# First image of an attention and feed-forward kernel: chunk-wise pipeline of four tiles, values turned from keys, staged weights, lag of three

## The chip, the cores and the metric

One core of one Trainium2 chip. The metric is the device time of one execution in microseconds; lower is better. "Span" is the time from the first to the last instruction in a profiled execution, about 2 us less than the device time. TensorE is called PE, VectorE DVE, ScalarE ACT, GpSimd POOL; SP is the engine that issues most DMAs. "Clock" is the share of TensorE's full speed that was granted, as a mean over the run or over a stretch; "half rate" is a time in which it was half. To "turn" is to transpose.

## The reference, cut to what matters

```python
# q (4, 12288, 128), kv (4, 384, 32, 128), w_sr (128, 128); all fp32
kv_pool = kv.reshape(B, H // 4, 4, W // 4, 4, C).mean(axis=(2, 4))   # 768 keys per image
k = v = kv_pool.reshape(B, -1, C) @ w_sr                             # keys and values are the same
a = softmax(q @ k.T / sqrt(128))                                     # per image
x = (a @ v).reshape(49152, 128)
out = (maximum(x @ w_gate, 0) * (x @ w_val)) @ w_out                 # hidden width 1536
```

The kernel works on 96 tiles of 512 tokens, 24 per image. The 768 keys of an image come in six chunks of 128, each pooled from 1.05 MB of kv. A tile needs 6 score matmuls, 24 value matmuls, 12 + 12 feed-forward projections and 48 output matmuls.

## The kernel before

First the start, for image 0. Each chunk is pooled (DVE), turned (PE), projected twice (once for keys, once for values, both in fp32) and scored against four tiles; values of two tiles follow one chunk later.

```python
def project(b, jc, kvT, copy):
    pr = bank([128, 2, 128])
    nc.tensor.matmul(pr[:, 0, :], w_sr_f32, kvT, start=True, stop=True)   # keys, channels by keys
    nc.tensor.matmul(pr[:, 1, :], kvT, w_sr_f32, start=True, stop=True)   # values, keys by channels
    copy(kv16[:, b, jc, 0 : 2 * C], pr.rearrange("p i c -> p (i c)"))

# start
for jc in range(NJC):                                    # NJC = 6
    s1 = pool_lines(nc.vector, 0, jc, nc.gpsimd if jc in (3, 4) else None)
    if jc == 3:
        q_load(1)                                        # second query group: casting DMA from GpSimd
    if jc == 4:
        # ... casting DMAs of w_val, w_gate, w_out, all from GpSimd ...
    if jc == 0:
        q_turn_pe(0)                                     # fp32 turns on PE
    kvT = turn_pooled(s1, nc.scalar.copy)
    if jc > 0:
        # ... values of tiles 0 and 1 for chunk jc - 1 ...
    project(0, jc, kvT, act_scaled)
    for k in range(GRP):                                 # GRP = 4
        if jc == 0 and k > 0:
            q_turn_pe(k)
        scores(k, jc)
q_turn(1)                                                # DMA transpose of the second query group
q_load(2)
# ... last values of tiles 0, 1; all values of tile 2; x_turn_pe(0), x_turn_pe(1) ...
for jc in range(NJC):
    scores(GRP, jc)                                      # needs the second query group
    values(3, jc, 0)
# ... rest of values of tile 3 ...
```

The main loop then works on tile k's scores, tile k - 1's values, the projections of tile k - LAG and the output of tile k - LAG - 1 at once, in 12 steps:

```python
for k in range(LEAD, last + 1):                          # LEAD = LAG = 5
    for step in range(NFB):                              # NFB = 12
        kO, kF = k - LAG - 1, k - LAG
        if 0 <= kO: out_proj(kO, step)
        if 0 <= kF < NT: value_proj(kF, step)
        # ... scores(k, ..) on even steps, values(k - 1, ..) on odd ones ...
        if 0 <= kF < NT: gate_proj(kF, step)
        # ... in the last tiles of an image: load, pool, turn and project the next image's chunks ...
```

The softmax here doesn't subtract the row's maximum and nothing guards it: scores larger than these inputs give would overflow.

Of the kernel before, what the change touches and what calls it, by code (L numbers as in the profile page):

```python
# [16 lines left out]
def kernel(  # L17
# [38 lines left out]
    LEAD = GRP + 1  # L56
    LAG = LEAD
# [39 lines left out]

    def q_turn_pe(i):
        q32 = q32s.pop(i)
        qt_ps = bank([128, NS, 128])  # L100
        for s in range(NS):
            nc.tensor.matmul(
                qt_ps[:, s, :], q32[:, s, :], ident, is_transpose=True, start=True, stop=True
            )
        if i == 0:
            qTs[0] = work.tile([128, GRP * NS, 128], FP16, tag="qT", bufs=3, name="qT")
        nc.vector.tensor_copy(qTs[0][:, i * NS : (i + 1) * NS, :], qt_ps)
# [21 lines left out]
    def pool_lines(eng, b, jc, other=None):  # L129
        parts = kv_in.pop((b, jc))  # L130
        s2 = work.tile([128, 2, r, C], FP32, tag="kv_s2")
        for i in range(2):
            (other if i and other else eng).tensor_tensor(  # L133
                s2[:, i], parts[:, 2 * i], parts[:, 2 * i + 1], op=ALU.add
            )
        s1 = work.tile([128, r, C], FP32, tag="kv_s1")
        eng.tensor_tensor(s1, s2[:, 0], s2[:, 1], op=ALU.add)  # L137
        return s1
# [8 lines left out]
    def turn_pooled(pooled, copy):  # L147
        tp = bank([128, 128])
        n = pooled.shape[1]
        for i in range(n):  # L150
            nc.tensor.matmul(  # L151
                tp, pooled[:, i, :], ident, is_transpose=True,
                start=(i == 0), stop=(i == n - 1),
            )
        kvT = work.tile([128, 128], FP32, tag="kvT")
        copy(kvT, tp)
        return kvT

    def project(b, jc, kvT, copy):
        pr = bank([128, 2, 128])  # L160
        nc.tensor.matmul(pr[:, 0, :], w_sr_f32, kvT, start=True, stop=True)  # L161
        nc.tensor.matmul(pr[:, 1, :], kvT, w_sr_f32, start=True, stop=True)  # L162
        copy(kv16[:, b, jc, 0 : 2 * C], pr.rearrange("p i c -> p (i c)"))

    def act_scaled(dst, src):
        nc.scalar.mul(dst, src, 1.0 / (r * r))

    def dve_scaled(dst, src):
        nc.vector.tensor_scalar(dst, src, 1.0 / (r * r), None, op0=ALU.mult)
# [5 lines left out]
    def scores(k, jc):  # L175
        if jc == 0:
            aTs[k] = work.tile([128, NJC, T], FP16, tag="aT", bufs=5, name="aT")
# [4 lines left out]
    def values(k, jc, half, turn=True):  # L182
# [13 lines left out]
        if jc == NJC - 1:  # L196
# [7 lines left out]
            if half == 1 and turn:  # L204
                x16 = x16s.pop(k)
                xT = work.tile([128, NS, 128], FP16, tag="xT", bufs=8, name="xT")
                nc.sync.dma_start_transpose(xT, x16.rearrange("p s c -> p (s c)"))
                xTs[k] = xT.rearrange("c s p -> c (s p)")

    def x_turn_pe(k):  # L210
# [4 lines left out]
        xT = work.tile([128, NS, 128], FP16, tag="xT", bufs=8, name="xT")  # L215
# [74 lines left out]
    wo16 = const.tile([128, NFB, 128], FP16)  # L290

    for jc in range(NJC):
        s1 = pool_lines(nc.vector, 0, jc, nc.gpsimd if jc in (3, 4) else None)
        if jc == 3:
            q_load(1)
        if jc == 4:
            for own in (slice(0, D_FF // 2), slice(D_FF // 2, D_FF)):
                nc.gpsimd.dma_start(wv16[:, own], moe_w_val[:, own])
                nc.gpsimd.dma_start(wg16[:, own], moe_w_gate[:, own])
            nc.gpsimd.dma_start(wo16, moe_w_out.rearrange("(fb f) c -> f fb c", f=128))  # L300
        if jc == 0:
            q_turn_pe(0)
        kvT = turn_pooled(s1, nc.scalar.copy)
        if jc > 0:
            for k in range(2):
                for half in range(2):
                    values(k, jc - 1, half, turn=False)
        project(0, jc, kvT, act_scaled)
        for k in range(GRP):
            if jc == 0 and k > 0:  # L310
                q_turn_pe(k)
            scores(k, jc)
    q_turn(1)
    q_load(2)
# [3 lines left out]
    for jc in range(NJC):  # L318
        values(2, jc, 0)
    for k in range(2):  # L320
        x_turn_pe(k)
    for jc in range(NJC):
        values(2, jc, 1)
    for jc in range(NJC):
        scores(GRP, jc)
        values(3, jc, 0)
    for jc in range(NJC):
        values(3, jc, 1)
# [4 lines left out]
    for k in range(LEAD, last + 1):  # L333
# [6 lines left out]
        for step in range(NFB):  # L340
            kO, kF = k - LAG - 1, k - LAG
            if 0 <= kO:
                out_proj(kO, step)
            if 0 <= kF < NT:
                value_proj(kF, step)
            if step % 2 == 0:
                if k < NT:
                    scores(k, step // 2)
            elif k - 1 < NT:
                half, i = divmod(step // 2, NJC // 2)  # L350
                values(k - 1, 2 * i, half)
                values(k - 1, 2 * i + 1, half)
            if 0 <= kF < NT:
                gate_proj(kF, step)
            if b < B:
# [4 lines left out]
                if step == 7 and 0 <= at - 4 < NJC:  # L360
                    kv_Ts[b, at - 4] = turn_pooled(kv_s3.pop((b, at - 4)), nc.vector.tensor_copy)
                if step == 9 and 0 <= at - 4 < NJC:
                    project(b, at - 4, kv_Ts.pop((b, at - 4)), dve_scaled)
# [34 lines left out]
```

## Time and profile before

| | before |
|---|---|
| device time, median of 4 runs | 1077.57 us (1073.12 to 1079.37) |
| span of the profiled run | 1071.8 us |
| first feed-forward matmul | 55.47 us |
| PE's wait for the turned second query group | 5.1 us, until 51.51 |
| one steady tile | 10.47 us, PE busy 10.47 |

The span consists of a start, in which PE has gaps, and a long rest, in which it has none. So the table is read as a sum: first feed-forward matmul at 55.47, and 1016.3 us from there. The lines for it stand in the prediction below; its 55.63 is where the chain of waits takes that matmul up, while PE's timeline has it start at 55.47. Two lines of the timeline of the kernel before (start, duration, engine, source line, operation, count, and in brackets the idle time before and what ended it) show how a chunk is paced there: the exponentials of four tiles come every 3.89 us.

```profile
30.94 2.06 ACT L180 ACTIVATE aT<-bank_ps 128x512 f16<-128x512 f32 x4 [0.48 <-PE bank_ps L179]
...
34.83 2.06 ACT L180 ACTIVATE aT<-bank_ps 128x512 f16<-128x512 f32 x4 [0.48 <-PE bank_ps L179]
```

2.06 us for four is the rate when PE delivers at full clock.

### The profile page before, as it was taken

The page shows a single profiled execution, that of the slowest core. Times are in us where ns is not written, and L with a number is a line of the kernel's source. Part 1 is how long each engine was busy: PE and PEld are TensorE (multiplying, and loading weights), DVE is VectorE, ACT ScalarE, POOL GpSimd, SP SyncE. Part 2 cuts the span into 40 slices and gives each one's busy share as a digit, 9 for nine tenths or more (in the row PEclk, how much of TensorE's full clock was granted, in tenths as well). Part 3 has the DMA queues.
Part 4 walks back from the last instruction along what each step waited for, and adds up shares of the span by engine and source line. Part 5 has one row for each costly group of instructions (what it writes and reads, how often), then busy time and mean ns, then how long its engine had stood idle before and what let it go on. Part 6 is the DMA issues. An engine that isn't in the chain of part 4 may idle for free.

```text
span 1071.8 us, 26152 instructions
## 1 busy us (share of the span) xinstructions
PE 1040.3 (97%) x9954; PEld 692.8 (65%) x9954; DVE 925.5 (86%) x1782; ACT 913.3 (85%) x1762; POOL 109.7 (10%) x128
## 2 busy tenths in 40 slices
PE   4699999999999999999999999999999999999997
PEld 2466666666666666666666666666666666666664
DVE  3388989898989889989888898988888889898896
ACT  1598888888888888888888888888888888888887
POOL 1200054200000015400000004420000000000000
PEclk9999999999999999999999999999999999999999
DMA  9953356341431447524313237643132232121111
GB/s 257 130 84 60 84 147 164 81 85 31 85 68 47 80 108 169 129 51 84 71 45 82 54 65 168 143 110 79 37 84 51 65 71 59 37 65 32 44 41 41
DMA packets 132911, 90.76 MB, mean 85 GB/s; under 512 B 104113, under 2 KB 104753, under 8 KB 132785
## 3 DMA queue, kind: packets, MB, share of 16 engines
q1 hardware_dynamic: 127344, 75.85, 31.3%
q0 software_dynamic: 5440, 13.24, 7.8%
q8 instruction: 78, 1.28, 0.5%
q14 instruction: 49, 0.39, 0.1%
HBM read 52.76 MB, written 25.17 MB: 73 GB/s over the span
## 4 chain that ended last, share of the span: by engine, by line
PE 94%; DMA 4%; ACT 0%; SPq 0%; DVE 0%; POOL 0%; issue 0%; ACTq 0%; POOLq 0%; DVEq 0%
PE bank_ps L246 24%; PE bank_ps L232 23%; PE bank_ps L221 23%; PE bank_ps L191 12%; PE bank_ps L179 11%; DMA parts<-in_kv_dram 2%; DMA qT<-q 2%; DMA q<-in_q_dram 1%; PE bank_ps L162 0%; PE bank_ps L161 0%; DVE hT L235 0%; PE bank_ps L151 0%; ACT o_sb L256 0%; POOL s L133 0%; SPq L124 0%
## 5 line engine op out<-in xcount | busy, mean ns | idle before, releaser
L235 DVE SCALAR_TENSOR_TENSOR hT<-bank_ps,val 128x512 f16<-128x512 f32 x1152 | 763.1, 686 | 102.0 <-ACT val L225 68.0
L225 ACT CAST val<-bank_ps 128x512 f16<-128x512 f32 x1152 | 677.4, 591 | 119.3 <-PE bank_ps L221 116.2
L246 PEld LDWEIGHTS <-hT 128*128 128x128 f16 x4608 | 351.8, 98 | 206.5 <-DVE hT L235 2.9
L246 PE MATMUL bank_ps<-wo,hT 128*128 128x128 f16 x4608 | 443.4, 219 | 2.1 <-DVE hT L235 2.0
L221 PE MATMUL bank_ps<-xT,wv 128*128 128x512 f16 x1152 | 436.6, 379 | 0.0
L232 PE MATMUL bank_ps<-xT,wg 128*128 128x512 f16 x1152 | 435.7, 378 | 0.3 <-DVE hT L235 0.3
L180 ACT ACTIVATE aT<-bank_ps 128x512 f16<-128x512 f32 x576 | 345.7, 604 | 15.8 <-PE bank_ps L179 15.7
L179 PE MATMUL bank_ps<-qT,kv 128*128 128x512 f16 x576 | 218.0, 383 | 10.3 <-DMA qT<-q 5.1
L191 PE MATMUL bank_ps<-kv,aT 128*128 128x129 f16 x2304 | 224.2, 220 | 0.1
L191 PEld LDWEIGHTS <-aT 128*128 128x128 f16 x2304 | 177.8, 98 | 68.1 <-issue 1.3
L232 PEld LDWEIGHTS <-wg 128*128 128x128 f16 x1152 | 111.5, 97 | 64.4
L221 PEld LDWEIGHTS <-wv 128*128 128x128 f16 x1152 | 112.7, 98 | 0.9 <-issue 0.5
L198 DVE CAST x<-bank_ps 128x256 f16<-128x256 f32 x192 | 79.4, 414 | 18.4 <-PE bank_ps L191 18.4
L78 POOL DMA_DIRECT2D q<-in_q_dram x23 | 12.7, 550 | 543.4 <-DMA qT<-q 543.2
L133 POOL TENSOR_TENSOR s<-parts 128x512 f32<-128x512 f32 x38 | 49.0, 1291 | 180.9 <-DMA parts<-in_kv_dram 119.0
L179 PEld LDWEIGHTS <-kv 128*128 128x128 f16 x576 | 56.4, 99 | 11.6 <-DMA qT<-q 5.2
L258 DVE TENSOR_TENSOR o_sb<-bank_ps,inv 128x512 f32<-128x512 f32 x91 | 61.9, 680 | 0.0
L199 DVE RECIPROCAL rinv<-bank_ps 128x2 f32<-128x2 f32 x192 | 30.5, 159 | 0.0
L137 POOL TENSOR_TENSOR s<-s 128x512 f32<-128x512 f32 x18 | 22.9, 1270 | 1.4
L203 DVE TENSOR_TENSOR inv<-rinv 128x4 f32<-128x4 f32 x96 | 19.0, 198 | 3.3
L133 DVE TENSOR_TENSOR s<-parts 128x512 f32<-128x512 f32 x10 | 8.8, 901 | 8.3 <-DMA parts<-in_kv_dram 8.3
L151 PE MATMUL bank_ps<-ident,s 128*128 128x128 f32 x42 | 9.7, 308 | 5.9 <-DVE s L137 5.7
(33 smaller groups left out, 108.9 us busy)
## 6 DMA issues: line engine op xcount, KB each, us to landing
parts<-in_kv_dram SPq DMA_DIRECT2D x96, 256.0 KB, 5.0
out_dram<-o_sb SPq DMA_DIRECT2D x96, 256.0 KB, 2.2
q<-in_q_dram POOLq DMA_DIRECT2D x23, 512.0 KB, 5.2
xT<-x SPq DMA_TRANSPOSE x94, 2.5
q<-in_q_dram SPq DMA_DIRECT2D x4, 256.0 KB, 5.9
wv<-in_moe_w_val_dram POOLq DMA_DIRECT2D x2, 192.0 KB, 5.4
wg<-in_moe_w_gate_dram POOLq DMA_DIRECT2D x2, 192.0 KB, 5.8
wo<-in_moe_w_out_dram POOLq DMA_DIRECT2D x1, 384.0 KB, 17.5
```

What stands on the lines that cost most here:

```text
L133: (other if i and other else eng).tensor_tensor(s2[:, i], parts[:, 2 * i], parts[:, 2 * i + 1], op=ALU.add)
L179: nc.tensor.matmul(s_ps, kv16[:, k // NST, jc, 0:C], qT_of(k), start=True, stop=True)
L180: nc.scalar.activation(aTs[k][:, jc, :], s_ps, AF.Exp, scale=qk_scale)
L191: nc.tensor.matmul(x_ps[:, i, :], aTs[k][:, jc, s * 128 : (s + 1) * 128], kv16[:, k // NST, jc, C : 2 * C + 1], start=(jc == 0 and i == 0) ...
L198: nc.vector.tensor_copy(x16s[k][:, own, :], x_ps[:, :, 0:C])
L199: nc.vector.reciprocal(rinvs[k][:, own], x_ps[:, :, C])
L221: nc.tensor.matmul(va_ps, wv16[:, fb * 128 : (fb + 1) * 128], xTs[k], start=True, stop=True)
L225: nc.scalar.copy(val, va_ps)
L232: nc.tensor.matmul(g_ps, wg16[:, fb * 128 : (fb + 1) * 128], xTs[k], start=True, stop=True)
L235: nc.vector.scalar_tensor_tensor(hTs[k][:, fb, :], g_ps, 0.0, vals.pop((k, fb)), op0=ALU.max, op1=ALU.mult)
L246: nc.tensor.matmul(o_ps[:, s, :], hTs[k][:, fb, s * 128 : (s + 1) * 128], wo16[:, fb, :], start=(fb == 0 and s == 0), stop=(fb == NFB - 1) ...
L258: nc.vector.tensor_tensor(o_sb, o_ps, inv2.to_broadcast([128, NS, 128]), op=ALU.mult)
```

## The change

Its intent is to let the feed-forward begin sooner. Image 0 runs chunk by chunk with the queries cast to fp16 on ACT before they are turned; one of the three additions that pool a chunk's lines goes to GpSimd (before, only for two chunks); keys alone are projected and the values are the same numbers turned by a cheap fp16 transpose; the weights come as plain fp32 DMAs from SP right behind kv and are cast by GpSimd; and the feed-forward starts when only four tiles are scored, with a lag of three instead of five. The core of the diff:

```diff
-    LEAD = GRP + 1
-    LAG = LEAD
+    LAG = GRP - 1
...
-    def project(b, jc, kvT, copy):
-        pr = bank([128, 2, 128])
-        nc.tensor.matmul(pr[:, 0, :], w_sr_f32, kvT, start=True, stop=True)
-        nc.tensor.matmul(pr[:, 1, :], kvT, w_sr_f32, start=True, stop=True)
-        copy(kv16[:, b, jc, 0 : 2 * C], pr.rearrange("p i c -> p (i c)"))
+    def project(b, jc, kvT):
+        pr = bank([128, 128])
+        nc.tensor.matmul(pr, w_sr_f32, kvT, start=True, stop=True)
+        nc.vector.tensor_scalar(
+            kv16[:, b, jc, 0:C], pr, 1.0 / (r * r), None, op0=ALU.mult
+        )
+    def turn_values(b, jc):
+        vt = bank([128, 128], FP16)
+        nc.tensor.transpose(vt, kv16[:, b, jc, 0:C], ident16)
+        nc.vector.tensor_copy(kv16[:, b, jc, C : 2 * C], vt)
...
+        w32 = work.tile([128, 2, HF], FP32, tag="kv_in", bufs=6, name="w32")
+        for n, (w16, w) in enumerate(((wv16, moe_w_val), (wg16, moe_w_gate))):
+            nc.sync.dma_start(w32[:, n], w[:, own])
...
     for jc in range(NJC):
-        s1 = pool_lines(nc.vector, 0, jc, nc.gpsimd if jc in (3, 4) else None)
+        s1 = pool_lines(nc.vector, 0, jc, nc.gpsimd)
+        kvT = turn_pooled(s1)
...     (values of tile 0 for chunk jc - 1)
+        project(0, jc, kvT)
...     (values of tile 1 for chunk jc - 1)
         for k in range(GRP):
             scores(k, jc)
+            if k == 0:
+                turn_values(0, jc)
+    q_load(1)
     q_turn(1)
+    for w16, w32 in staged:
+        nc.gpsimd.tensor_copy(w16, w32)
     q_load(2)
...
+            if k == LAG:                    # first feed-forward tile: values of tiles 2 and 3
+                for jc in (2 * i, 2 * i + 1):
+                    values(k - 1 + step % 2, jc, half)
```

More of the change, by code (lines that the diff above doesn't have):

```diff
@@ L96, in q_load_plain, with q_cast @@
         q32s[i] = q32
+    def q_cast(i):
+        q16 = work.tile([128, NS, C], FP16, tag="q16s", bufs=2, name="q16s")
+        nc.scalar.copy(q16, q32s[i])
+        q16s[0, i] = q16
     def q_turn_pe(i):
-        q32 = q32s.pop(i)
-        qt_ps = bank([128, NS, 128])
+        q16 = q16s.pop((0, i))
+        qt_ps = bank([128, NS, 128], FP16)
         for s in range(NS):
-            nc.tensor.matmul(
-                qt_ps[:, s, :], q32[:, s, :], ident, is_transpose=True, start=True, stop=True
-            )
+            nc.tensor.transpose(qt_ps[:, s, :], q16[:, s, :], ident16)
         if i == 0:
@@ L132, in pool_lines @@
         for i in range(2):
-            (other if i and other else eng).tensor_tensor(
+            (other if i == 0 and other else eng).tensor_tensor(
                 s2[:, i], parts[:, 2 * i], parts[:, 2 * i + 1], op=ALU.add
@@ L145, in pool_columns, with turn_pooled @@
         return s3
-    def turn_pooled(pooled, copy):
+    def turn_pooled(pooled):
         tp = bank([128, 128])
@@ L155, in turn_pooled @@
         kvT = work.tile([128, 128], FP32, tag="kvT")
-        copy(kvT, tp)
+        nc.vector.tensor_copy(kvT, tp)
         return kvT
-    def project(b, jc, kvT, copy):
-        pr = bank([128, 2, 128])
-        nc.tensor.matmul(pr[:, 0, :], w_sr_f32, kvT, start=True, stop=True)
-        nc.tensor.matmul(pr[:, 1, :], kvT, w_sr_f32, start=True, stop=True)
-        copy(kv16[:, b, jc, 0 : 2 * C], pr.rearrange("p i c -> p (i c)"))
-    def act_scaled(dst, src):
-        nc.scalar.mul(dst, src, 1.0 / (r * r))
-    def dve_scaled(dst, src):
-        nc.vector.tensor_scalar(dst, src, 1.0 / (r * r), None, op0=ALU.mult)
+    def project(b, jc, kvT):
[8 more added lines that the diff above has]
+        nc.vector.tensor_copy(kv16[:, b, jc, C : 2 * C], vt)
     aTs, x_banks, x16s, xTs, rinvs, inv2s = {}, {}, {}, {}, {}, {}
@@ L176, in scores @@
         if jc == 0:
-            aTs[k] = work.tile([128, NJC, T], FP16, tag="aT", bufs=5, name="aT")
+            aTs[k] = work.tile([128, NJC, T], FP16, tag="aT", bufs=4, name="aT")
         s_ps = bank([128, T])
@@ L205, in values @@
                 x16 = x16s.pop(k)
-                xT = work.tile([128, NS, 128], FP16, tag="xT", bufs=8, name="xT")
+                xT = work.tile([128, NS, 128], FP16, tag="xT", bufs=5, name="xT")
                 nc.sync.dma_start_transpose(xT, x16.rearrange("p s c -> p (s c)"))
@@ L214, in x_turn_pe @@
             nc.tensor.transpose(xt_ps[:, s, :], x16[:, s, :], ident16)
-        xT = work.tile([128, NS, 128], FP16, tag="xT", bufs=8, name="xT")
+        xT = work.tile([128, NS, 128], FP16, tag="xT", bufs=5, name="xT")
         nc.vector.tensor_copy(xT, xt_ps)
@@ L290 @@
     wo16 = const.tile([128, NFB, 128], FP16)
-    for jc in range(NJC):
-        s1 = pool_lines(nc.vector, 0, jc, nc.gpsimd if jc in (3, 4) else None)
-        if jc == 3:
-            q_load(1)
-        if jc == 4:
-            for own in (slice(0, D_FF // 2), slice(D_FF // 2, D_FF)):
-                nc.gpsimd.dma_start(wv16[:, own], moe_w_val[:, own])
-                nc.gpsimd.dma_start(wg16[:, own], moe_w_gate[:, own])
-            nc.gpsimd.dma_start(wo16, moe_w_out.rearrange("(fb f) c -> f fb c", f=128))
-        if jc == 0:
-            q_turn_pe(0)
-        kvT = turn_pooled(s1, nc.scalar.copy)
-        if jc > 0:
-            for k in range(2):
-                for half in range(2):
-                    values(k, jc - 1, half, turn=False)
-        project(0, jc, kvT, act_scaled)
+    HF = D_FF // 2
+    staged = []
+    for i in range(2):
+        own = slice(i * HF, (i + 1) * HF)
+        w32 = work.tile([128, 2, HF], FP32, tag="kv_in", bufs=6, name="w32")
+        for n, (w16, w) in enumerate(((wv16, moe_w_val), (wg16, moe_w_gate))):
+            nc.sync.dma_start(w32[:, n], w[:, own])
+            staged.append((w16[:, own], w32[:, n]))
+    w32 = work.tile([128, NFB, 128], FP32, tag="kv_in", bufs=6, name="w32")
+    nc.sync.dma_start(w32, moe_w_out.rearrange("(fb f) c -> f fb c", f=128))
+    staged.append((wo16, w32))
+    q_cast(0)
+    q_turn_pe(0)
+    for jc in range(NJC):
+        s1 = pool_lines(nc.vector, 0, jc, nc.gpsimd)
+        kvT = turn_pooled(s1)
+        if jc == 0:
+            for i in range(1, GRP):
+                q_cast(i)
+        else:
+            values(0, jc - 1, 0, turn=False)
+            values(0, jc - 1, 1, turn=False)
+        project(0, jc, kvT)
+        if jc == 0:
+            for i in range(1, GRP):
+                q_turn_pe(i)
+        else:
+            values(1, jc - 1, 0, turn=False)
+            values(1, jc - 1, 1, turn=False)
         for k in range(GRP):
-            if jc == 0 and k > 0:
-                q_turn_pe(k)
             scores(k, jc)
+            if k == 0:
+                turn_values(0, jc)
+    q_load(1)
     q_turn(1)
+    for w16, w32 in staged:
+        nc.gpsimd.tensor_copy(w16, w32)
     q_load(2)
@@ L317 @@
             values(k, NJC - 1, half, turn=False)
-    for jc in range(NJC):
-        values(2, jc, 0)
-    for k in range(2):
-        x_turn_pe(k)
-    for jc in range(NJC):
-        values(2, jc, 1)
-    for jc in range(NJC):
-        scores(GRP, jc)
-        values(3, jc, 0)
-    for jc in range(NJC):
-        values(3, jc, 1)
+    x_turn_pe(0)
     last = NT + LAG - 1
     kv_s3, kv_Ts = {}, {}
-    for k in range(LEAD, last + 1):
+    for k in range(LAG, last + 1):
         g, ph = divmod(k, GRP)
@@ L341 @@
             kO, kF = k - LAG - 1, k - LAG
+            half, i = divmod(step // 2, NJC // 2)
             if 0 <= kO:
                 out_proj(kO, step)
-            if 0 <= kF < NT:
+            if kF < NT:
                 value_proj(kF, step)
-            if step % 2 == 0:
+            if k == LAG:
+                for jc in (2 * i, 2 * i + 1):
+                    values(k - 1 + step % 2, jc, half)
+            elif step % 2 == 0:
                 if k < NT:
                     scores(k, step // 2)
-            elif k - 1 < NT:
-                half, i = divmod(step // 2, NJC // 2)
+            elif k > GRP and k - 1 < NT:
                 values(k - 1, 2 * i, half)
                 values(k - 1, 2 * i + 1, half)
-            if 0 <= kF < NT:
+            if kF < NT:
                 gate_proj(kF, step)
+            if k == LAG and step == 2:
+                x_turn_pe(1)
             if b < B:
@@ L359 @@
                     kv_s3[b, at - 2] = pool_columns(nc.gpsimd, pool_lines(nc.gpsimd, b, at - 2))
-                if step == 7 and 0 <= at - 4 < NJC:
-                    kv_Ts[b, at - 4] = turn_pooled(kv_s3.pop((b, at - 4)), nc.vector.tensor_copy)
-                if step == 9 and 0 <= at - 4 < NJC:
-                    project(b, at - 4, kv_Ts.pop((b, at - 4)), dve_scaled)
+                if 0 <= at - 4 < NJC:
+                    if step == 5:
+                        kv_Ts[b, at - 4] = turn_pooled(kv_s3.pop((b, at - 4)))
+                    if step == 7:
+                        project(b, at - 4, kv_Ts.pop((b, at - 4)))
+                    if step == 9:
+                        turn_values(b, at - 4)
             if k == last and step >= 2:
```

## The prediction

> **What bounds the kernel now.** I read the page first: shares of engines, then the 40 slices, then the chain that ended last.
>
> ```profile
> span 1071.8 us, 26152 instructions
> PE 1040.3 (97%) x9954; PEld 692.8 (65%) x9954; DVE 925.5 (86%) x1782; ACT 913.3 (85%) x1762; POOL 109.7 (10%) x128
> ...
> PE   4699999999999999999999999999999999999997
> PEld 2466666666666666666666666666666666666664
> ...
> PE 94%; DMA 4%; ACT 0%; SPq 0%; DVE 0%; POOL 0%; issue 0%; ACTq 0%; POOLq 0%; DVEq 0%
> ```
>
> PE carries 94% of the last chain, DMA the other 4%. A slice is 26.8 us: only the first two (4 and 6 tenths) and the last (7) are not full. Is the middle truly full? The table of stretches, over 10.47 us in the middle of the run, answers:
>
> ```profile
> 300.00:310.47 10.47, 10.47 (x105) 6.93 (x103) 9.35 (x19) 9.34 (x19) 0.00 (x0) 1.00 0.13 38
> ```
>
> One tile of 512 tokens needs, by starts in the timeline, 12+12+6 matmuls of 512 columns at 0.2155 us, 24 of 129 columns at 0.056 and 48 of 128 columns at 0.0555: 6.47 + 1.35 + 2.66 = 10.48 us. So a steady tile has no bubble to remove; DVE and ACT (9.35 and 9.34 us) lie just under it. Ninety-six tiles make 1006 us, and 18 key chunks of the three later images some 12 more. The rest, about 54 us of 1072, is mostly the start. The chain of waits from 24 us on shows what the start ends with:
>
> ```profile
> 23.03 1.52 POOL s L133
> 24.55 7.88 DMA q<-in_q_dram
> 32.45 19.02 DMA qT<-q
> 51.51 0.61 PE bank_ps L179
> ...
> 55.63 0.22 PE bank_ps L221
> ```
>
> The second group of queries is fetched only at 24.55, its DMA transpose takes 19.02 us because it shares the engines with the weights and the third group (other transposes of this tile land in 4.3 to 4.6), and PE stands still for 5.1 us until 51.51. The first feed-forward matmul (L221) starts at 55.63. Before that, attention of the first image is served at one key chunk per 3.89 us (exponentials of chunk starts at 30.94, 34.83, 38.72, 42.61), while kv lands at a chunk of 1.05 MB per 3.65 us (288 GB/s in the stretches from 3 to 30 us). The columns PE, DVE, ACT, POOL of the starting stretches show that no engine is full there:
>
> ```profile
> 10.00:20.00 10.00, 6.46 (x23) 4.59 (x24) 3.04 (x5) 2.44 (x5) 0.00 (x0) 1.00 1.06 283
> ...
> 31.00:43.00 12.00, 8.90 (x63) 5.32 (x61) 1.02 (x2) 8.15 (x19) 1.11 (x2) 1.00 1.38 137
> ```
>
> **What the skill says.** "TensorE: Matmul & The Clock Gate", section "Wait — 56ns, not 53.3ns?": warm matmuls of 128 and 512 columns start 55.6 and 215.7 ns apart; the trace agrees (0.0555, 0.2155), so the middle is at its floor. The same page, "What's actually happening": the array starts, and restarts after some 3.4 us of idling, at half rate. The trace agrees: scores take 0.61 us at 14.3 and again at 51.5, 0.38 otherwise. "DMA: Bandwidth & Descriptors", section "SWDGE vs HWDGE vs iDMA": a DMA that casts must come from GpSimd; a plain one may come from SP. That is why the change fetches weights as fp32 and casts on GpSimd. "GPSIMD Engine Reference", section 3.1: the best one-input loop does 512 elements in 769 ns. The trace has only a 128-column cast (0.29 us), which agrees roughly; from both, I estimate 1.2 to 1.7 us for 768 columns and 2.3 to 3.4 for 1536.
>
> **The change part by part.** The question is when the first feed-forward matmul starts, and how much work is then left.
>
> 1. Chunk 0. Its last lines land at 9.67. DVE adds twice (2 x 0.69), PE turns (1.1 cold), DVE copies (0.28), PE projects (0.75 cold), DVE scales (0.28): 13.7. Twelve fp16 query transposes (12 x 0.107 = 1.3) now lie together, and their DVE copies from fp16 take 0.41 (as the 128x512 fp16 copy L216) instead of 0.69. First scores near 14.6, values turned and copied by 15.5. Before, four query turns in fp32 held DVE until 20.9.
>
> 2. Each later chunk. In the order of DVE's instructions of the changed kernel, a chunk's additions stand behind the previous chunk's value copy; so it is one serial chain: add 0.69, add 0.69, turn 0.66, copy 0.28, project 0.49, scale 0.28, scores and value turn 0.22 + 0.28, copy 0.2, handoffs 0.3: 4.1 us warm, about 4.9 cold. GpSimd's addition of the other half (1.27) is done ahead. The chain, not the kv stream, sets this phase: ends at 15.5, 20.4, 24.7, 28.8, 32.9, **37.0**. Against 3.89 per chunk before this is a slower period from a much earlier start.
>
> 3. From there to the feed-forward: scores of chunk 5 start at 36.3, exponential ends at 37.3, values, two tiles' casts and reciprocals (1.09 us each, as at 43.59 before), copy of the turned tile 0.41: first feed-forward matmul at about **40.2**, not 55.6.
>
> 4. Weights: 7.4 MB of queries and kv at 0.288 MB/us end near 28.6; the weights' first halves land near 32 to 33 and are cast by 36.5, the second halves by 40 (needed at about 45), the output weights by 44 (needed at 50). Hidden. The second query group is fetched near 29, turned by about 43, and needed only one tile after the start, near 50: the 19 us wait goes.
>
> 5. Work left at the start of the feed-forward. Before, 5 tiles were scored and 4 had values; now 4 and 2: + 6 x 0.2155 + 2 x 1.35 = +4.0 us. Eighteen fp32 projections go (18 x 0.22 = 3.9), eighteen transposes come (18 x 0.056 = 1.0): -2.9 us.
>
> 6. The first feed-forward tile now carries values of two tiles. DVE needs 12 x 0.605 (its pitch in the last tiles) + 4 x 0.52 + 0.7 = 10.0 us there, PE only 7.87: PE loses about 2.4 us, of which about 0.5 existed before (ACT full from 56.6 to 64).
>
> 7. Lag of three. The final tiles run at 0.655 us per step, which is PE's own pace (2 x 0.2155 + 4 x 0.0555), so fewer of them save nothing. A turned tile has one full tile, 10 us, for a DMA of 2.5 us: no new wait.
>
> Sum: -15.4 + 4.0 - 2.9 + 1.9 = **-12.4 us**, 1.15%. From the median, 1077.65, this gives 1065.3.
>
> **The rivals.** (a) The kv stream sets the start, with the chunk chain shorter than I think (value copies overlapping the next additions): then the last chunk ends near 32 and the feed-forward starts near 35; about 1060. For it: 288 GB/s was sustained. Against: DVE's order puts the copy first. (b) The second query group again comes late, because weights, third group and transpose meet in the same queues: PE waits 5 us or so at the second tile; 1070. For it: exactly this happened before, and all weights are now ahead of the transpose in SP's queue. Against: it now has some 20 us from fetch to need. (c) PE stays at half rate through the chunks (about 50% busy in step 2): +0.8 us for each of four chunks; 1068. (d) Less lag and fewer buffers make small bubbles in the middle: 0.1 us per tile would eat 10 us; 1075. Against: no wait over 0.3 us of PE shows in the middle now.
>
> **Range and chances.** The uncertain terms are the chain (+-4 us), a query stall (0 to 5) and run to run spread (1073 to 1079 before). I take 1056 to 1073. Over 2% faster needs -21.5 us, a feed-forward start at 31, before the kv stream with its chain can end: 5%. Slower by 2% needs bubbles in the middle: 1%. Within 2%: 94%.
>
> **What would show it.** First feed-forward matmul between 37 and 43 us; exponentials of successive chunks about 4.1 us apart; DVE nearly full in the following 10 us and PE at some 80%; no wait on the turned queries over 1 us; a steady tile still 10.47 us. A start of the feed-forward outside 35 to 45, a wait for weights there, or a longer steady tile would make me wrong.

## The result, and the profile after

The changed kernel takes 1064.80 us (median of 4 runs, 1062.81 to 1068.04) against 1077.57. The ratio is 0.989 with a 95% interval of 0.985 to 0.993; ratios here are the mean time of one kernel's runs over that of the other's in the same rounds, so not quite the ratio of the medians. Another chip gave 1065.69 and 0.993. The result lies in the predicted range, half a microsecond from the predicted 1065.3. Page of the changed kernel: span, engines, and the chain that ended last.

```profile
span 1063.1 us, 26203 instructions
PE 1035.9 (97%) x9930; PEld 688.5 (65%) x9930; DVE 929.3 (87%) x1816; ACT 910.8 (86%) x1746; POOL 115.9 (11%) x132
...
PE 96%; DVE 2%; DMA 1%; issue 0%; ACT 0%; SPq 0%; ACTq 0%; DVEq 0%
```

DMA's share of the chain fell from 4% to 1%, and 2% of DVE came in: the wait for the query transpose is gone, and the start now hangs on the pooling. Next, the timeline of ACT's exponentials in the changed kernel, one line per chunk (2.06 us for four is the rate when PE delivers at full clock; 2.11 is seen where PE delivers at half of it):

```profile
15.45 2.11 ACT L182 ACTIVATE aT<-bank_ps 128x512 f16<-128x512 f32 x4 [1.12 <-PE bank_ps L181]
19.86 2.06 ACT L182 ACTIVATE aT<-bank_ps 128x512 f16<-128x512 f32 x4 [2.30 <-PE bank_ps L181]
24.06 2.06 ACT L182 ACTIVATE aT<-bank_ps 128x512 f16<-128x512 f32 x4 [2.13 <-PE bank_ps L181]
28.31 2.11 ACT L182 ACTIVATE aT<-bank_ps 128x512 f16<-128x512 f32 x4 [2.19 <-PE bank_ps L181]
34.46 2.11 ACT L182 ACTIVATE aT<-bank_ps 128x512 f16<-128x512 f32 x4 [4.04 <-PE bank_ps L181]
39.49 2.11 ACT L182 ACTIVATE aT<-bank_ps 128x512 f16<-128x512 f32 x4 [2.93 <-PE bank_ps L181]
```

And from PE's timeline the first feed-forward matmul (L223) and the first output matmul (L248):

```profile
44.18 0.38 PE L223 MATMUL bank_ps<-xT,wv 128*128 128x512 f16 x1 [1.92 <-DVE xT L218]
...
53.96 0.39 PE L248 MATMUL bank_ps<-wo,hT 128*128 128x128 f16 x4
```

The first four chunks follow at 4.4, 4.2 and 4.25 us, as foreseen; the fifth and sixth come after 6.15 and 5.03. The feed-forward starts at 44.18: 11.3 us sooner than before, not 15.4. From there the span has 1018.9 us left (the prediction's terms give 1016.3 + 4.0 - 2.9 + 1.9 = 1019.3). What makes the two late chunks is seen in the timeline of all engines (lines of other engines left out):

```profile
28.56 0.68 DVE L135 TENSOR_TENSOR s<-parts 128x512 f32<-128x512 f32 x1
...
29.14 1.26 POOL L135 TENSOR_TENSOR s<-parts 128x512 f32<-128x512 f32 x1 [2.29 <-DMA parts<-in_kv_dram]
29.35 1.60 DVE L139 TENSOR_TENSOR s<-s 128x512 f32<-128x512 f32 x1
...
31.10 1.09 PE L153 MATMUL bank_ps<-ident,s 128*128 128x128 f32 x4 [1.44 <-DVE s L139]
```

An addition of 0.69 us took 1.60 because GpSimd had begun one 0.2 us sooner, and the turn after it took 1.09 us instead of 0.63, because PE had fallen back to half rate: two causes in one chunk. The table of stretches (length; busy time of PE, its weight load, DVE, ACT, POOL; granted clock; DMA share; GB/s) shows the second over time, and that a steady tile is unchanged:

```profile
20.00:30.00 10.00, 6.62 (x41) 3.37 (x39) 5.59 (x13) 5.67 (x12) 3.64 (x3) 0.90 1.06 273
30.00:40.00 10.00, 7.15 (x37) 4.57 (x38) 4.39 (x9) 3.04 (x6) 4.42 (x6) 0.67 1.19 292
40.00:50.00 10.00, 8.00 (x54) 5.03 (x53) 6.41 (x19) 4.76 (x10) 2.48 (x3) 0.75 0.75 145
...
300.00:310.47 10.47, 10.47 (x104) 6.93 (x102) 9.55 (x20) 9.34 (x19) 0.00 (x0) 1.00 0.16 43
```

The clock of 0.67 and 0.75 between 30 and 50 us is the half rate for part of the time. (The column does not show the half rate at the very start: it has 1.00 from 10 to 20 us, where the exponentials at 15.45 took 2.11.)

Both causes could be seen in the trace of the kernel before, and the prediction passed over them. Its score matmuls at 16.56, 18.78 and 21.00 took 0.58 to 0.59 us, so PE was still at half rate at 21 us; and one of DVE's additions already took 1.76 us beside one of GpSimd's (from the timeline of all engines):

```profile
26.62 1.81 POOL L133 TENSOR_TENSOR s<-parts 128x512 f32<-128x512 f32 x1 [1.38 <-DVE s L133]
...
27.22 1.76 DVE L133 TENSOR_TENSOR s<-parts 128x512 f32<-128x512 f32 x1
```

### The profile page after: what moved, and what is told of

Read it like the earlier page. It is cut to its first block, busy times and chain, and to the rows that moved or that the text cites. A ratio compares the mean times of both kernels' runs of the same rounds, so it can differ in the third digit from the quotient of the medians. Undisturbed runs are those within 1.5% of the kernel's fastest.

```text
span 1063.1 us, 26203 instructions
## 1 busy us (share of the span) xinstructions
PE 1035.9 (97%) x9930; PEld 688.5 (65%) x9930; DVE 929.3 (87%) x1816; ACT 910.8 (86%) x1746; POOL 115.9 (11%) x132
## 3 DMA queue, kind: packets, MB, share of 16 engines
q8 instruction: 77, 1.26, 0.5%
## 4 chain that ended last, share of the span: by engine, by line
PE 96%; DVE 2%; DMA 1%; issue 0%; ACT 0%; SPq 0%; ACTq 0%; DVEq 0%
PE bank_ps L248 24%; PE bank_ps L234 23%; PE bank_ps L223 23%; PE bank_ps L193 12%; PE bank_ps L181 12%; PE bank_ps L163 1%; PE bank_ps L153 1%; DMA parts<-in_kv_dram 1%; DVE s L139 1%; DVE s L135 0%; DVE hT L237 0%; SPq L126 0%; DVE x L200 0%; PE bank_ps L170 0%; ACT o_sb L258 0%
## 5 line engine op out<-in xcount | busy, mean ns | idle before, releaser
L248 PEld LDWEIGHTS <-hT 128*128 128x128 f16 x4608 | 351.1, 98 | 206.2 <-DVE hT L237 2.9
L248 PE MATMUL bank_ps<-wo,hT 128*128 128x128 f16 x4608 | 443.4, 219 | 2.1 <-DVE hT L237 2.0
L223 PE MATMUL bank_ps<-xT,wv 128*128 128x512 f16 x1152 | 437.1, 379 | 1.9 <-DVE xT L218 1.9
L193 PE MATMUL bank_ps<-kv,aT 128*128 128x129 f16 x2304 | 226.5, 221 | 0.0
L223 PEld LDWEIGHTS <-wv 128*128 128x128 f16 x1152 | 112.8, 98 | 0.0
L135 POOL TENSOR_TENSOR s<-parts 128x512 f32<-128x512 f32 x42 | 53.5, 1274 | 191.1 <-DMA parts<-in_kv_dram 184.0
L153 PEld LDWEIGHTS bank_ps<-ident,s 128*128 128x128 f32 x42 | 5.8, 160 | 13.3 <-ACT aT L182 7.5
```

The source lines that it names most:

```text
L135: (other if i == 0 and other else eng).tensor_tensor(s2[:, i], parts[:, 2 * i], parts[:, 2 * i + 1], op=ALU.add)
L193: nc.tensor.matmul(x_ps[:, i, :], aTs[k][:, jc, s * 128 : (s + 1) * 128], kv16[:, k // NST, jc, C : 2 * C + 1], start=(jc == 0 and i == 0) ...
L223: nc.tensor.matmul(va_ps, wv16[:, fb * 128 : (fb + 1) * 128], xTs[k], start=True, stop=True)
L248: nc.tensor.matmul(o_ps[:, s, :], hTs[k][:, fb, s * 128 : (s + 1) * 128], wo16[:, fb, :], start=(fb == 0 and s == 0), stop=(fb == NFB - 1) ...
```

## The experiments

Eleven runs followed (ten variants, and the changed kernel once more), on three chips, each timed against the kernel before on its own chip. One trace was taken of each. "FF" is the first feed-forward matmul, "OUT" the first output matmul, both from that trace.

| run | FF us | OUT us | span us | median us | ratio to before (95%) |
|---|---|---|---|---|---|
| before | 55.47 | 63.77 | 1071.8 | 1077.57 | 1 |
| after | 44.18 | 53.96 | 1063.1 | 1064.80 | 0.989 (0.985 to 0.993) |
| b_staged | 48.12 | 56.70 | 1065.1 | 1068.92 | 0.993 (0.991 to 0.994) |
| b_lag4 | 46.73 | 61.12 | 1074.0 | 1075.17 | 0.999 (0.997 to 1.001) |
| b_staged_lag4 | 46.63 | 54.93 | 1067.8 | 1068.70 | 0.994 (0.992 to 0.996) |
| a_two_proj | 39.12 | 47.24 | 1059.5 | 1063.69 | 0.988 (0.986 to 0.990) |
| a_pool_ahead | 38.63 | 48.41 | 1057.4 | 1059.33 | 0.984 (0.982 to 0.985) |
| a_warm | 41.50 | 49.64 | 1059.6 | 1061.88 | 0.988 (0.986 to 0.990) |
| a_pool_busy | 49.85 | 57.97 | 1067.1 | 1070.39 | 0.996 (0.993 to 0.998) |
| a_ahead_early | 36.98 | 45.10 | 1053.6 | 1058.62 | 0.984 (0.982 to 0.986) |
| after_again | 44.96 | 54.75 | 1065.3 | 1065.69 | 0.993 (0.991 to 0.995) |
| a_swdge | 43.79 | 53.67 | 1070.3 | 1067.70 | 0.995 (0.992 to 0.997) |
| a_best | 37.78 | 45.90 | 1056.5 | 1059.53 | 0.987 (0.985 to 0.989) |

The kernel before itself had medians of 1077.03, 1075.45 and 1073.94, so medians differ by some 3 us for no reason of the kernels.

### Parts of the change, alone in the kernel before

**b_staged**: only the weights are done in the new way.

```diff
 (kernel before)
-            # casting DMAs of the weights from GpSimd after chunk 4
+    # fp32 DMAs of the weights from SP behind kv, into the buffers of kv
     q_turn(1)
+    for w16, w32 in staged:
+        nc.gpsimd.tensor_copy(w16, w32)
     q_load(2)
```

> Only the weights are done in the new way in the kernel before: fetched as fp32 by SP behind kv, cast by GpSimd after the additions. My theory: the 19.0 us landing of the second query group came from weights, third group and transpose sharing the DMA engines, so with the weights ahead of it the transpose lands before 46 us, the 5.1 us wait of PE at 51.5 goes, the feed-forward starts near 50 instead of 55.6 and the span falls by 5 to 6.5 us from 1071.8. Rival: the transpose is held anyway because it now stands behind the weights in SP's queue; then the wait stays at 4 us or more and the time moves by less than 1.5 us.

It gained 8.1 us (1068.92 against 1077.03), more than the 5 to 6.5 that were written. The slowest of this tile's transposes now lands in 8.2 us instead of 19.0, PE never waits for it, and the feed-forward starts at 48.12. The excess is probably the clock: after its wait of 5.1 us the kernel before works at half rate from 51.5 to about 54.3, and this run doesn't (clock 0.998 to 1.000 in its five runs, against 0.995 to 0.997 in nearly all of the kernel before). The rival (the transpose is held behind the weights) is refuted. Staging changes three things at once (the weights move earlier, SP issues them, and nothing is cast on the way); which of them frees the transpose, no run separates.

This one part reaches a ratio of 0.993. The whole change has 0.989 and 0.993: the feed-forward then starts sooner still, at 44.18 and 44.96, but with more work left (1018.9 us from there against 1017.0), so these runs do not settle that the rest of the change adds to staging.

**b_lag4**: only the lag is shortened, to the four that this start allows.

```diff
-    LEAD = GRP + 1
+    LEAD = GRP
...
-    for jc in range(NJC):
-        scores(GRP, jc)
-        values(3, jc, 0)
-    for jc in range(NJC):
-        values(3, jc, 1)
```

> Only the lag is shortened in the kernel before, from five tiles to four, the smallest that its start allows. My theory: the lag by itself is worth nothing, since the tiles at the end run at PE's own pace and the wait for the turned queries merely moves into the first feed-forward tile: time within 1 us of before, first feed-forward matmul near 46.5, then a stop of PE until about 51.5. Rival: a shorter pipe saves its fill and drain, some 8 us for one tile.

Ratio 0.999: nothing. PE's timeline of this run shows where the earlier start went: the first feed-forward matmul runs at 46.73, and the first scores of the next tile wait for the same transpose.

```profile
51.07 0.61 PE L179 MATMUL bank_ps<-qT,kv 128*128 128x512 f16 x1 [3.96 <-DMA qT<-q]
```

**b_staged_lag4**: both together.

> Kernel before with weights staged and lag of four tiles together. My theory: with the wait for the turned queries gone, the shorter lag lets the feed-forward start right after the first two tiles are turned, near 45.5 instead of 48.1, but the scores and values of two more tiles are then still to be done, so nothing more is gained than from the staged weights alone: within 1.5 us of that run (1068.9). Rival: lag and staging support each other and it comes near the changed kernel (1064.8 or less).

1068.70, as with staging alone (1068.92; ratios 0.994 and 0.993). The feed-forward starts 1.5 us sooner, but the rest is longer, 1067.8 - 46.63 = 1021.2 us against 1065.1 - 48.12 = 1017.0. One more tile's scores and values are left at that moment (not two, as the expectation had it), 6 x 0.2155 + 1.35 = 2.6 us; the other 1.6 are not explained, and near the spread of such sums from trace to trace. Starting PE on other work earlier gives nothing when PE was not idle before.

### Parts of the change, undone in the changed kernel

**a_swdge**: the weights and the second query group are fetched as in the kernel before, everything else stays.

```diff
 (changed kernel)
         s1 = pool_lines(nc.vector, 0, jc, nc.gpsimd)
+        if jc == 3:
+            q_load(1)
+        if jc == 4:
+            # casting DMAs of the weights from GpSimd
...
-    for w16, w32 in staged:
-        nc.gpsimd.tensor_copy(w16, w32)
```

> Changed kernel with the weights fetched as before: by GpSimd DMAs that cast, issued after the additions of chunk 4, and the second query group after chunk 3; no staging, no casts on GpSimd. My theory: staging is what moved the kernel before (8 us there), but here the turned queries are wanted only one tile after the feed-forward starts, so their late landing near 50 is hidden: within 1.5 us of the changed kernel, perhaps 0.5 faster since GpSimd leaves DVE alone. Rival: transpose and weights meet as before, PE waits 2 us or more for the turned queries or for the output weights, and the time is 3 us or more above the changed kernel.

The expectation missed. In the traced run PE waited for the output weights and then for the turned queries, and after that worked at half rate (0.61 for a score matmul); the transpose took 25.1 us to land:

```profile
53.67 0.40 PE L248 MATMUL bank_ps<-wo,hT 128*128 128x128 f16 x4 [1.60 <-DMA wo<-in_moe_w_out_dram]
53.91 0.38 PE L223 MATMUL bank_ps<-xT,wv 128*128 128x512 f16 x1
57.13 0.61 PE L181 MATMUL bank_ps<-qT,kv 128*128 128x512 f16 x1 [2.85 <-DMA qT<-q]
```

Its runs scatter from 1063.62 to 1072.04 (the changed kernel beside it: 1064.32 to 1068.91), with a median 2.0 us above. The two intervals overlap, so the cost on average is small and not settled; what is shown is that the two waits exist in the traced run, the slowest of the six, and that the traces with staging have neither.

**a_two_proj**: values by a second fp32 projection again.

```diff
-        pr = bank([128, 128])
+        pr = bank([128, 2, 128])
+        nc.tensor.matmul(pr[:, 1, :], kvT, w_sr_f32, start=True, stop=True)
...
-            if k == 0:
-                turn_values(0, jc)
```

> Changed kernel with values computed by a second fp32 projection again, instead of being turned from the keys. My theory: the middle gains 18 x 0.22 - 18 x 0.056 = 2.9 us of PE work, while in the start the value copy leaves the serial chain of a chunk (4.2 us to about 3.8), which brings the feed-forward start forward by 1 to 2 us from 44.2; in sum 1 to 2 us slower than the changed kernel. Rival: turning is hidden or free in the start, then 3 us slower; or the start is all that counts, then faster.

This missed as well, and taught more than a hit. The middle behaved as computed: from the first output matmul on, this run needs 1059.5 - 47.24 = 1012.3 us, the changed kernel 1063.1 - 53.96 = 1009.1 (six other traces with the same main loop and staged weights 1008.5 to 1010.6; the mean of the seven is 1009.6, so 2.7 more against 2.9 computed). But the start gained 5.1 us, not 1 to 2: the chunk period fell to 3.79 us as foreseen, and all six sets of exponentials took 2.06 or 2.07, so PE never fell back to half rate. Turning the values, the part that saves PE work in the middle, costs as much or more in the start. Two things differ there, the value copy that stood in DVE's order between a chunk and the next one, and PE's rate; this run alone does not divide the 5.1 us between them. In device time it can't be told from the changed kernel (ratio 0.988 against 0.989 and 0.993).

### The serial chain, the clock and GpSimd

**a_pool_ahead**: the additions of the next chunk are put on DVE right after a chunk is scaled.

```diff
+    s1 = pool_lines(nc.vector, 0, 0, nc.gpsimd)
     for jc in range(NJC):
-        s1 = pool_lines(nc.vector, 0, jc, nc.gpsimd)
         kvT = turn_pooled(s1)
...
         project(0, jc, kvT)
+        if jc + 1 < NJC:
+            s1 = pool_lines(nc.vector, 0, jc + 1, nc.gpsimd)   # after the query turns for jc == 0
```

> Changed kernel with one move: the two additions of chunk c+1 are put on DVE right after the scaling of chunk c, ahead of its value copy, so that they no longer close a serial chain. My theory: the period falls from 4.2 to about 3.6 us and the kv stream, whose last lines land near 31 us, sets the end of the chunks; feed-forward starts near 39 instead of 44.2; 5 us faster than the changed kernel (span about 1058). Rival: PE's and ACT's own order sets the period, then less than 1.5 us.

Feed-forward at 38.63, 1059.33 us, ratio 0.984: the chain of step 2 is real, and breaking it starts the feed-forward 5.5 us sooner. The period of the middle chunks is 3.48 us. Part of the 5.5 may be the clock: with the shorter period PE kept its full rate in the last four chunks (exponentials of 2.06). It fell back only afterwards, in the first feed-forward tile, which the table of stretches of this run shows and which will matter below:

```profile
40.00:50.00 10.00, 10.00 (x82) 6.29 (x80) 8.62 (x21) 7.11 (x13) 2.34 (x3) 0.85 0.82 145
```

**a_warm**: filler matmuls, results unread, so that PE is busier.

```diff
+    def fill(n):
+        f_ps = bank([128, T])
+        for _ in range(n):
+            nc.tensor.matmul(f_ps, ident16, qTs[0][:, 0:NS, :].rearrange("c s p -> c (s p)"), start=True, stop=True)
...
+        fill(4)          # at the end of each chunk
...
     x_turn_pe(0)
+    fill(6)
```

> Changed kernel with filler matmuls whose result nobody reads: four of 512 columns at the end of each chunk, where PE waits for DVE anyway, and six before the first feed-forward matmul. My theory: the half rate that PE falls back to from 28 us on costs about 1.3 us in chunk 4, 0.5 in chunk 5, 0.5 before the feed-forward and 1.7 in its first steps, together some 3 to 4 us; with the filler no matmul is at half rate after 20 us, the feed-forward starts near 42 and the runs lie at 1060 to 1062 with less spread. Rival: PE's rate is not on the path there (DVE and GpSimd are); then within 1 us of the changed kernel, or slower by the filler.

Exponentials of the sixth chunk come at 37.19 instead of 39.49, feed-forward at 41.50 instead of 44.18, and the clock is 1.000 in the traced run, 0.998 to 0.999 in the others, against 0.992 to 0.998 in ten runs of the changed kernel. Two lines from ACT's timeline of this run show the even period:

```profile
28.64 2.06 ACT L182 ACTIVATE aT<-bank_ps 128x512 f16<-128x512 f32 x4 [2.13 <-PE bank_ps L181]
32.84 2.06 ACT L182 ACTIVATE aT<-bank_ps 128x512 f16<-128x512 f32 x4 [2.13 <-PE bank_ps L181]
```

Work that nobody needs lets the feed-forward start 2.7 us sooner, and the span of the traced run is 3.5 us below that of the changed kernel's. The interval of the ratio, 0.986 to 0.990, lies inside the changed kernel's first one (0.985 to 0.993) and below its second (0.991 to 0.995), so the gain in device time is less sure than the mechanism. Two side results: the first feed-forward tile takes 49.64 - 41.50 = 8.14 us here and 8.12 in a_two_proj, against 9.78 in the changed kernel; and DVE's second addition of chunk 4 is back at 0.69, since here it begins just before GpSimd's (29.63 against 29.76 us) and GpSimd's is the one held, at 1.69 us instead of 1.26.

**a_pool_busy**: the contention made larger.

```diff
         s1 = pool_lines(nc.vector, 0, jc, nc.gpsimd)
+        for _ in range(2):
+            nc.gpsimd.tensor_tensor(z_out, z_in, z_in, op=ALU.add)   # scratch, read by nobody
```

> Changed kernel with the suspected contention made larger: after its addition for each chunk GpSimd does two more additions of 128x512 fp32 on scratch, read by nobody (GpSimd some 3.8 of the 4.2 us of a chunk busy). My theory: DVE's two-input additions, 0.69 us alone and up to 1.60 beside GpSimd, are then held in every chunk; the feed-forward starts 4 to 8 us later than 44.2. Rival: the long additions at 29.35 and 35.59 had another cause (a late kv line); then DVE's additions stay at 0.69 and the start moves by less than 1 us.

Feed-forward at 49.85, 5.7 us later, inside the 4 to 8 expected. Seven of DVE's twelve additions took longer than 0.8 us, five of them 1.03 to 1.61, and in one place GpSimd's casts followed each other so closely that DVE did not get in for several of them. From DVE's timeline of this run, and then from GpSimd's:

```profile
35.20 3.68 DVE L139 TENSOR_TENSOR s<-s 128x512 f32<-128x512 f32 x1
```

```profile
35.19 0.84 POOL L336 CAST wv<-w 128x768 f16<-128x768 f32 x1
35.96 0.83 POOL L336 CAST wg<-w 128x768 f16<-128x768 f32 x1
36.73 0.83 POOL L336 CAST wv<-w 128x768 f16<-128x768 f32 x1
37.51 0.82 POOL L336 CAST wg<-w 128x768 f16<-128x768 f32 x1
38.39 1.81 POOL L336 CAST wo<-w 128x1536 f16<-128x1536 f32 x1
```

The Trainium skill, page "SBUF — State Buffer", section "Who interferes with whom", says that a DVE instruction with two SBUF inputs contends with a GpSimd instruction that reads SBUF, and that the ports they share are an exclusive lock. These lines agree. Part of the 5.7 us is not DVE's: the clock of this run is 0.993, and GpSimd's own additions came later behind the extra ones.

**after_again**: the changed kernel on the third chip.

> The changed kernel itself once more, beside the next two on the same chip. My theory: as before, 1063 to 1066, ratio 0.987 to 0.991, mean granted clock 0.992 to 0.996 with the half rate in the last chunks showing again, since its cause is how little PE has to do per chunk. Rival: the half rate was chance; then a clock of 0.998 or more and a feed-forward start near 41.5.

Its trace shows the half rate again (clock 0.992; exponentials of 2.11 in four of six chunks) and a feed-forward start at 44.96, so the first trace was no accident. Over the ten runs of this kernel the clock and the time go together: 1064.4 us on average in the three runs at 0.998, 1067.3 in the four at 0.992 or 0.993.

### Looking for a faster version

**a_ahead_early**: additions ahead, and the first tile is turned and copied before the second tile's values are cast.

```diff
-    for k in range(2):
-        for half in range(2):
-            values(k, NJC - 1, half, turn=False)
-    x_turn_pe(0)
+    for half in range(2):
+        values(0, NJC - 1, half, turn=False)
+    x_turn_pe(0)
+    for half in range(2):
+        values(1, NJC - 1, half, turn=False)
```

> Changed kernel with additions one chunk ahead, and with the first tile turned and copied before the second tile's values are cast. My theory: the copy of the turned tile moves ahead of 1.1 us of DVE work, so the feed-forward starts near 37.5 instead of 38.6, but DVE is what limits the first feed-forward tile and has the same work left, so the span falls by 0.5 us or less. Rival: a full 1.1 us.

1058.62 us, ratio 0.984, the same as a_pool_ahead: no further gain in time that the runs resolve, though the traced run (the fastest, 1055.38) starts at 36.98. In that trace DVE waits for kv before most chunks, which shows the next bound:

```profile
18.99 0.69 DVE L135 TENSOR_TENSOR s<-parts 128x512 f32<-128x512 f32 x1 [0.18 <-DMA parts<-in_kv_dram]
...
22.76 0.69 DVE L135 TENSOR_TENSOR s<-parts 128x512 f32<-128x512 f32 x1 [0.31 <-DMA parts<-in_kv_dram]
...
26.39 0.69 DVE L135 TENSOR_TENSOR s<-parts 128x512 f32<-128x512 f32 x1 [0.17 <-DMA parts<-in_kv_dram]
...
30.26 0.69 DVE L135 TENSOR_TENSOR s<-parts 128x512 f32<-128x512 f32 x1 [0.41 <-DMA parts<-in_kv_dram]
```

The spacing is 3.6 to 3.9 us, the pace at which 1.05 MB arrive.

**a_best**: the same with two filler matmuls per chunk.

> Additions one chunk ahead, first tile turned early, and two filler matmuls per chunk, all in the changed kernel. My theory: the kv stream sets the start (last lines near 31 us), feed-forward starts near 37 and PE is at full rate after 20 us; 1057 to 1059, 6 to 8 us below the changed kernel on this chip. Rival: the filler costs as much as it gives: then as without it (1058.6) or slower.

1059.53 us; on the same chip the changed kernel took 1065.69, so 6.2 us less. Against a_ahead_early (another chip, 0.984 to 0.987) the filler gives nothing, as the rival had it: with the chain broken the clock is 0.997 to 1.000 in the five runs without it. Both have shorter times than the changed kernel: a_best on its own chip, a_ahead_early by its ratio (0.982 to 0.986, against 0.985 to 0.993 and 0.991 to 0.995).

## Why the prediction was right

The time, the range and the verdict were right, and so was the mechanism: the gain is the earlier start of the feed-forward, less the work that is then still to be done. Of its announced signs, though, three failed: the feed-forward started at 44.18, outside 37 to 43 (and, at 44.96 in the second trace, just inside the limit of 45 that would have made it wrong), the last two chunks did not come about 4.1 us apart, and DVE was not nearly full in the first tile. By its own steps:

- **Chunk 0 and the chain of later chunks (1 and 2)**: right. 15.5 was computed for the end of chunk 0 and DVE began the next additions at 15.70; 4.1 us per warm chunk was computed, 4.2 measured (in the second trace, largely at half rate, 5.2 to 5.6 for four of the five, where about 4.9 was computed). a_pool_ahead shows that the chain, not the kv stream, sets the pace, and a_ahead_early that the stream is next, as rival (a) had it.
- **End of the chunks and start of the feed-forward (2 and 3)**: mis-sized. 37.0 and 40.2 became 39.8 and 44.18. The term "4.1 us warm" was applied to the last two chunks, which took 6.15 and 5.03. Two causes are shown: PE at half rate, which rival (c) named with 0.8 us in each of four chunks (a_warm starts 2.7 us sooner), and DVE held by GpSimd, which no step or rival named (a_pool_busy starts 5.7 us later); the prediction said only that GpSimd's addition was done ahead. Its reading of the score matmuls, "0.38 otherwise", left out those of 0.58 to 0.59 us before 22 us. In the trace the held instructions exceed their usual length by 0.9, 0.1, 0.4 and 0.6 us (the additions at 29.35, 34.71 and 35.59, and the small multiplication at 42.03 beside the cast of the output weights), 2.0 together. The two don't simply add: at full rate, in a_warm, GpSimd lost the collision of chunk 4 and not DVE.
- **Weights and queries (4)**: right. The first half began to land at 32.1 and was cast by 34.0; the casts took 0.82 to 0.89 and 1.47 us, less than the 1.2 to 1.7 and 2.3 to 3.4 estimated; the queries were turned at about 43. Rival (b) did not come true; without the staging, in the traced run of a_swdge, PE did wait 2.85 us for the queries.
- **Work left (5)**: right in size. With step 6 it gave 3.0 us more after the start of the feed-forward than before; the traces have 1018.9 - 1016.3 = 2.6. Of these 1.5 are the longer first tile (9.78 against 8.30 before), which leaves 1.1, as step 5 has it (4.0 - 2.9); the spread between traces, up to 2 us, is larger than such an agreement. Its term for the projections, 2.9, is 2.7 by a_two_proj.
- **The first feed-forward tile (6)**: the step that failed in its reason. 10.0 us were computed because DVE would limit it, and 9.78 were measured. (The stated loss of 2.4 us is also a little more than 10.0 - 7.87 = 2.1.) But DVE was busy for only 7.40 of these 9.78 us and PE for all of them, at a clock of 0.83: PE's timeline has matmuls at half rate from 45.05 to 48.45. With PE at full rate the same instructions take 8.12 to 8.14 (a_two_proj, a_warm, a_pool_busy, a_ahead_early, a_best), and in a_pool_ahead and after_again, where PE falls back again, 9.78 and 9.79. So PE's half rate made the difference, and the DVE work that the prediction put into this tile is in part done in the next one (there DVE was busy for 9.97 of 10.47 us). A right number with a wrong cause.
- **Lag (7)**: right; b_lag4 is worth nothing. A steady tile stayed at 10.47 us with three tiles of lag, so rival (d) fell.

The sum in spans is -8.7 where -12.4 was predicted; the medians differ by 12.8 because the traced run of the kernel before was one of its fast ones (1073.74 against a median of 1077.57). The close hit of the median owes something to that luck: span against span the sum is 3.7 us short. The ten runs of the changed kernel against two chips' runs of the kernel before give 0.989 and 0.993, that is a gain of 0.7 to 1.1%; 1.15% was predicted.

Seen by parts, either half alone gives much of the gain: 0.993 with staging only (b_staged), 0.995 with all but the staging and the new order of the query fetch (a_swdge), 0.989 and 0.993 with both. They overlap, so their gains must not be added.

What stays open: what in the staging frees the transpose, why a_swdge scatters over 8 us, and why the part after the start differs by up to 2 us (1008.5 to 1010.6) between traces with the same main loop.

## What to carry to other kernels

When the steady part is at its floor, write the time as "start of the steady part" plus "work left at that moment": a change that only moves work across that line, like a shorter lag or an earlier first matmul, gives nothing unless it fills idle PE time. In a serial start, look at the order on the in-order engines: an instruction that saves work everywhere can cost more than it saves if it closes a chain between one chunk and the next, and moving two additions was worth more here than any other single edit to the changed kernel. (In the kernel before, staging the weights alone gained 8.1 us.) Where PE has short work and many short waits, check the clock before blaming another engine for a long tile.

## What the Trainium skill lacked or had wrong

- "TensorE: Matmul & The Clock Gate": the part on warming up says when PE falls back by naming idle gaps of some 3.4 us; the section "A second HAM failure mode: psum-queue depth-cycling" says that short idles can do it too, but gives no measure. Here PE fell back at 28 us in the changed kernel, with no idle gap over 1.2 us in the 8 us before. An estimate from the traces: PE's work per chunk at full rate is 4 x 0.115 + 0.22 + 8 x 0.056 + 4 x 0.2155 + 0.056 = 2.05 us, 49% of the period of 4.2. At 55% (a_ahead_early, 2.05 of 3.73), 57% (kernel before, 2.21 of 3.89), 58% (a_two_proj, 2.21 of 3.79) and 69% (a_warm, 2.91 of 4.2) it stayed at full rate through the later chunks. Without the turns the shares are 36% against 41, 45, 46 and 57, so the order is the same; the runs do not show which count matters, nor where between them a limit lies.
- "GPSIMD Engine Reference", section 3.1: it doesn't say which of its rates a cast has. The 769 ns for 512 elements, which it calls the best case and the prediction took, are too long: 128 columns took 0.29 us, 768 took 0.82 and 1536 took 1.47, so about 0.18 us fixed and 0.84 ns per column. Its other figure, 1.03 cycles per element at the 1.2 GHz that it divides by (0.86 ns), fits. The estimate was up to 2.3 times too long; half of it scaled the 128-column cast without taking off the fixed part.
- "SBUF — State Buffer", section "Who interferes with whom": right for one collision (0.69 us became 1.60). It does not say that a queue of GpSimd instructions can keep DVE out for several of them in a row: 3.68 us beside casts of 0.83 us each.
- No page gives what a DMA transpose takes beside casting DMAs of the weights: 19.0 us in the kernel before and 25.1 in a_swdge, against a median of 4.6 and 4.4 for all transposes of this tile.
